# Where four reductions and four PSUM evacuations stand among the first FFN chunks of a gated-mix kernel

## The chip, the cores and the metric

The kernel runs on one core of one Trainium2 chip. The metric is the device time of one execution in microseconds. The median of four runs before the change is 179.18 us, from 178.49 to 179.32. One more execution was taken with the hardware profiler; every line of a profile in this text comes from that execution, and its times count from the start of its span.

Five engines work side by side, each through its own instructions in order: TensorE (PE), which multiplies matrices into PSUM, VectorE (DVE), ScalarE (ACT), GpSimd (POOL) and SyncE (SP), whose queue starts most of the transfers. They wait for each other by semaphores. Weight loads of PE are listed apart as PEld.

## The reference

For 2048 tokens x of width 512, a linear attention block a and a gated FFN b are mixed per token:

```python
x = A_x
g = _sigmoid((x * gate_w).sum(-1, keepdims=True))
a = _A_ref(x, A_wqkv, A_wo)
b = _B_ref(x, B_w1, B_w3, B_w2)
return g * a + (1 - g) * b
```

The attention has 32 heads of 16, with phi(t) = t + 1 where t > 0 and exp(t) elsewhere, plus 1e-6. It is linear: `kv` is the sum over tokens of phi(k) times v, `z` the sum of phi(k), and the output `o` of a token is `num / den`, with `num` = phi(q) times kv and `den` = phi(q) times z for each head, followed by the product with `wo`. The FFN is silu(x w1) * (x w3), times w2, with 1376 hidden units.

## The kernel before

Tokens are cut into four blocks of 512 (`tb` 0 to 3), each into four tiles of 128 (`tt`). The hidden units are ten chunks of 128 (`fc` 0 to 9) and a remainder of 96. The work has three stages.

First, for all 16 tiles, phi(k) is made (`emit_k`) and the products XP of x and phi(k) are added up in four PSUM banks, tags XP0 to XP3 of the pool psX. POOL adds up the phi(k) tiles (`pks`), from which z is made.

Second, block 0 is prepared, in the part around the change: phi(q) (`emit_q`, tiles `pq`), the remainder (`emit_rem`), the small matrix `kvT_sb`, and from it W, the product of kv and wo. PE makes W in the four psX banks as `W_ps0` to `W_ps3`, between chunk 1 and chunk 2 of the FFN; ACT copies them to `W_sb` with a scale (L476).

Third, for each block: ten FFN chunks, then per tile the output `emit_out`, among which the next block's `emit_q`, `emit_rem` and `emit_den` are placed, and then `emit_norm` for that next block.

One FFN chunk (`emit_ffn`, from L312) is: four matmuls gate_ps (L322) and four matmuls up_ps (L330) on PE, `th` = tanh of half of gate_ps on ACT (L335), `gs` = (th + 1) * gate_ps on DVE (L337), and `hT` = up_ps * gs on DVE (L342). A function given as `between` is called between gs and hT.

PSUM sets what waits for what. The pool psM has four banks, which gate_ps and up_ps take in turn: chunk 2 takes again what chunk 0 had, chunk 3 what chunk 1 had. A gate_ps is free when th and gs have read it, an up_ps when hT has. In block 0, chunks 4 and 6 don't use psM but the psX banks, by the table in L317: chunk 4 takes XP2 and XP3, so `W_ps2` and `W_ps3` must have been evacuated before it, and chunk 6 takes XP0 and XP1, so `W_ps0` and `W_ps1` before that. Chunk 5 then takes chunk 2's banks, chunk 7 chunk 3's, chunk 8 chunk 5's and chunk 9 chunk 7's.

The denominator (`emit_den`, L226) is, per tile, a product qz of pq and z on POOL (L228), into one of three buffers, and a reduction to 32 sums on DVE (L231). `emit_norm` (L281) makes rden from the four sums of a block with three DVE operations (L284, L287, L288), then eight products pqn on POOL (L297, three buffers) and four transposing transfers on SP's queue into pqT (L307). The first matmuls of each output tile (L363) read pqT and W_sb.

The order on PE is written out throughout (`manual_schedule`, L153). On DVE it is written out from L414 to L476, which covers chunks 0 to 2 of block 0; behind that, and on the other engines, a scheduler places the instructions. `emit_norm(0)` is called after chunk 5 (L480), and the scheduler puts its three DVE operations at the gs and hT of chunks 3 and 4.

Of the kernel before, what the change touches and what calls it, by code (L numbers as in the profile page):

```python
# [8 lines left out]
ACT = mybir.ActivationFunctionType  # L9
ALU = mybir.AluOpType  # L10
AX = mybir.AxisListType
ENG = mybir.EngineType
FP32 = mybir.dt.float32
# [4 lines left out]
def kernel(  # L18
# [12 lines left out]
    nc = tc.nc  # L31
    P = nc.NUM_PARTITIONS

    Bb, S, D = A_x.shape
# [7 lines left out]
    TPB = TB // P  # L42
    FC = F // P
# [5 lines left out]
    NG = P // G  # L49
# [41 lines left out]
        out=xT[:, :, TF * P : TB], in_=x2d[TF * P : TB, :], transpose=True  # L91
    )
    for tb in range(1, NTB):
        dq.dma_start(
            out=xT[:, :, tb * TB : (tb + 1) * TB], in_=x2d[tb * TB : (tb + 1) * TB, :],
# [7 lines left out]
    with nc.allow_non_contiguous_dma(reason="one gate weight per partition and chunk"):  # L103
        dq.dma_start(
            out=wr_sb[:, :, 2 * FR : NR], in_=gate_w.rearrange("(kc d o) -> d kc o", d=P, o=1)
        )
    dq.dma_start(out=wv_sb[:], in_=wqkv_r[:, :, 2 * D : 3 * D])
    for fsl in (slice(0, FM // 2), slice(FM // 2, FM)):
# [13 lines left out]
        out=bm, in_=bm, pattern=[[-Dh, HPC], [0, Dh]], compare_op=ALU.is_ge, fill=0.0,  # L122
# [3 lines left out]
        out=bm, in_=bm, pattern=[[Dh, HPC], [0, Dh]], compare_op=ALU.is_ge, fill=0.0,  # L126
# [4 lines left out]
    W_sb = consts.tile([P, KC, D], BF16, name="W_sb")  # L131
# [24 lines left out]
    psX = ctx.enter_context(tc.tile_pool(name="psX", bufs=1, space=bass.MemoryType.PSUM))  # L156
# [55 lines left out]
    def emit_q(tb, tt, pool, tag):  # L212
        t = tb * TPB + tt
        ts_tok = slice(t * P, (t + 1) * P)
        if tt == 0:
            st[tb, "pq"] = blk.tile([P, TPB, D], BF16, tag="pq", name="pq")
            st[tb, "den"] = blk.tile([P, TPB, H], FP32, tag="den", name="den")
        q_ps = pool.tile([P, D], FP32, tag=tag, name="q_ps")
        for kc in range(KC):
            nc.tensor.matmul(  # L220
                q_ps[:], lhsT=xT[:, kc, ts_tok], rhs=wq_sb[:, kc, :],
                start=(kc == 0), stop=(kc == KC - 1),
            )
        phi(st[tb, "pq"][:, tt, :], q_ps[:])

    def emit_den(tb, tt):  # L226
        qz = work.tile([P, D], FP32, tag="qz", name="qz")
        nc.gpsimd.tensor_tensor(  # L228
            out=qz[:], in0=st[tb, "pq"][:, tt, :], in1=z_sb[:], op=ALU.mult
        )  # L230
        nc.vector.tensor_reduce(  # L231
            out=st[tb, "den"][:, tt, :], in_=qz[:].rearrange("p (h d) -> p h d", d=Dh),
            axis=AX.X, op=ALU.add,
        )
# [38 lines left out]
    def emit_omg(tb):  # L273
        om = work.tile([P, TPB], FP32, tag="om", name="om")
        nc.vector.tensor_scalar(  # L275
            out=om[:], in0=st[tb, "el"][:], scalar1=2.0, scalar2=2.0, op0=ALU.mult,
            op1=ALU.add,
        )
        nc.vector.reciprocal(out=omg[:, tb * TPB : (tb + 1) * TPB], in_=om[:])
# [32 lines left out]
    def emit_ffn(tb, fc, between=None):  # L312
        tok_sl = slice(tb * TB, (tb + 1) * TB)
        fsl = slice(fc * P, (fc + 1) * P)
        if fc == 0:
            st[tb, "hT"] = blk.tile([P, FC, TB], BF16, tag="hT", name="hT")
        aside = {4: ("XP2", "XP3"), 6: ("XP0", "XP1")}.get(fc) if tb == 0 else None  # L317
        gate_ps = (psX if aside else psM).tile(
            [P, TB], FP32, tag=aside[0] if aside else "mm", name="gate_ps"
        )  # L320
        for kc in range(KC):
            nc.tensor.matmul(  # L322
                gate_ps[:], lhsT=w1_sb[:, kc, fsl], rhs=xT[:, kc, tok_sl],
                start=(kc == 0), stop=(kc == KC - 1),
            )
        up_ps = (psX if aside else psM).tile(
            [P, TB], FP32, tag=aside[1] if aside else "mm", name="up_ps"
        )
        for kc in range(KC):
            nc.tensor.matmul(  # L330
                up_ps[:], lhsT=w3_sb[:, kc, fsl], rhs=xT[:, kc, tok_sl],
                start=(kc == 0), stop=(kc == KC - 1),
            )
        th = work.tile([P, TB], BF16, tag="th", name="th")
        nc.scalar.activation(out=th[:], in_=gate_ps[:], func=ACT.Tanh, scale=0.5)  # L335
        gs = work.tile([P, TB], BF16, tag="gs", name="gs")
        nc.vector.scalar_tensor_tensor(  # L337
            out=gs[:], in0=th[:], scalar=1.0, in1=gate_ps[:], op0=ALU.add, op1=ALU.mult
        )
        if between:  # L340
            between()
        nc.vector.tensor_tensor(  # L342
            out=st[tb, "hT"][:, fc, :], in0=up_ps[:], in1=gs[:], op=ALU.mult
        )
# [69 lines left out]
    with tc.manual_schedule(engines={ENG.DVE}):  # L414
        Q = 32
        NB = D // Q
        zt = consts.tile([P, NB, Q], FP32, name="zt")
        nc.vector.transpose(out=zt[:].rearrange("p b f -> p (b f)"), in_=pks[:])
        w = Q // 2
        while w >= 1:  # L420
            nc.gpsimd.tensor_add(zt[:, :, 0:w], zt[:, :, 0:w], zt[:, :, w : 2 * w])
            w //= 2
        zq = zt[:, :, 0]
        z_up = consts.tile([P // 2, NB], FP32, name="z_up")
        z_h = consts.tile([P // 2, NB], FP32, name="z_h")
        z_hi = consts.tile([Q, NB], FP32, name="z_hi")
        z_col = consts.tile([P, NB], FP32, name="z_col")
        nc.gpsimd.tensor_copy(z_up[:], zq[P // 2 : P, :])
        nc.gpsimd.tensor_add(z_h[:], zq[0 : P // 2, :], z_up[:])
        nc.gpsimd.tensor_copy(z_hi[:], z_h[Q : 2 * Q, :])  # L430
        for b in range(P // Q):
            nc.gpsimd.tensor_add(z_col[b * Q : (b + 1) * Q, :], z_h[0:Q, :], z_hi[:])
        for dc in range(KC):
            if dc % 2 == 0:
                nc.scalar.activation(out=XP_sb[:, dc, :], in_=XP_ps[dc][:], func=ACT.Copy)
            else:
                nc.vector.tensor_copy(out=XP_sb[:, dc, :], in_=XP_ps[dc][:])

        emit_q(0, TPB - 1, psM, "mm")
        emit_rem(0, 0, psM, "mm")  # L440
        emit_rem(0, 1, psM, "mm")
        nc.vector.transpose(
            out=z_sb[:].rearrange("p (b f) -> p b f", f=Q),
            in_=z_col[:, :, None].to_broadcast([P, NB, Q]),
        )
        kvT_ps = psX.tile([P, KC, P], FP32, tag="XP0", name="kvT_ps")
        for c in range(KC):
            csl = slice(c * P, (c + 1) * P)
            for dc in range(KC):
                nc.tensor.matmul(  # L450
                    kvT_ps[:, c, :], lhsT=wv_sb[:, dc, csl], rhs=XP_sb[:, dc, csl],
                    start=(dc == 0), stop=(dc == KC - 1),
                )
        nc.vector.tensor_tensor(
            out=kvT_sb[:], in0=kvT_ps[:],
            in1=blockmask[:, None, :].to_broadcast([P, KC, P]), op=ALU.mult,
        )

        emit_omg(0)
        for fc in range(3):  # L460
            if fc == 0:
                emit_ffn(0, fc)
                continue
            emit_den(0, 2 * fc - 2)
            emit_ffn(0, fc, between=lambda: emit_den(0, 2 * fc - 1))
            if fc == 1:
                W_ps = [psX.tile([P, D], FP32, tag=f"XP{i}", name=f"W_ps{i}") for i in range(NG)]
                for i in range(NG):
                    gsl = slice(i * G, (i + 1) * G)
                    for c in range(KC):  # L470
                        nc.tensor.matmul(
                            W_ps[i][c * G : (c + 1) * G, :], lhsT=kvT_sb[gsl, c, gsl],
                            rhs=wo_sb[gsl, c, :], start=True, stop=True,
                        )
            for i in ((2, 3) if fc == 1 else (0, 1)):
                nc.scalar.activation(out=W_sb[:, i, :], in_=W_ps[i][:], func=ACT.Copy, scale=2.0)  # L476

    for fc in range(3, FC):
        emit_ffn(0, fc)
        if fc == TPB + 1:  # L480
            emit_norm(0)
# [47 lines left out]
```

## Time and profile before

| What | Value |
| --- | --- |
| median of four runs | 179.18 us |
| runs | 178.49, 179.17, 179.32, 179.19 us |
| the profiled execution | 179.29 us |
| its span, first to last instruction | 177.6 us |
| mean granted TensorE clock | 0.998 of full speed |
| DVE reductions L231 | 16, 684 ns each |
| ACT evacuations of W, L476 | 4, 603 ns each |
| ACT tanh L335 | 40, 598 ns each |
| POOL products L228 / L297 | 16, 1160 ns each / 32, 626 ns each |

The profiled execution lasts 1.69 us longer than its span, which counts from the first to the last instruction. Busy time of an engine is the sum of its instructions' lengths; instructions of one engine can overlap at their ends, since one starts before the last one's result is written. So the distance from start to start says how fast an engine goes on, and the length says when a result is there.

The span in 40 slices of 4.4 us shows how full each engine is, in tenths:

```profile
PE   8999999999999999999999999999999999999994
DVE  0397667899999837498786375978754669786000
ACT  3542323476442334343333333342443333331222
POOL 6087765689155323263003232720032328100000
```

Chunks 0 to 9 of block 0 lie from 38.7 to 56.9 us, slices 9 to 13 (counted from 1), where DVE is at nine tenths or more.

### The profile page before, as it was taken

The numbers are of one execution on the slowest core, as the hardware profiler recorded it, in microseconds if no ns is written. First come the engines' busy times: TensorE is split into PE (matmuls) and PEld (weight loads), VectorE is DVE, ScalarE is ACT, GpSimd is POOL, SyncE is SP. The second block draws the span as 40 slices with busy tenths as digits, with TensorE's granted clock in tenths as the row PEclk, the third lists the DMA queues.
The fourth block names the chain that finished last, engine by engine and source line by source line (L and its number), as shares of the span: only waits on it lengthen the run. The fifth ranks groups of instructions, "written<-read, shape, count | busy, mean of one in ns | idle before, by whom it ended". The sixth has DMA issues, their size and how long they took to land.

```text
span 177.6 us, 2513 instructions
## 1 busy us (share of the span) xinstructions
PE 174.0 (98%) x895; PEld 83.8 (47%) x895; DVE 118.6 (67%) x204; ACT 65.3 (37%) x123; POOL 66.2 (37%) x96
## 2 busy tenths in 40 slices
PE   8999999999999999999999999999999999999994
PEld 4444444474444545444454544444545444444463
DVE  0397667899999837498786375978754669786000
ACT  3542323476442334343333333342443333331222
POOL 6087765689155323263003232720032328100000
PEclk9999999999999999999999999999999999999999
DMA  5999999901004010123000111240001012300002
GB/s 181 243 283 241 279 363 362 339 24 22 17 0 111 7 48 30 44 59 89 0 4 7 37 37 37 59 94 2 0 7 55 23 51 63 70 0 0 30 33 59
DMA packets 30380, 15.14 MB, mean 85 GB/s; under 512 B 20928, under 2 KB 30240, under 8 KB 30368
## 3 DMA queue, kind: packets, MB, share of 16 engines
q1 hardware_dynamic: 29952, 14.67, 29.8%
q10 hardware_dynamic: 416, 0.31, 0.6%
q8 instruction: 7, 0.11, 0.3%
q14 instruction: 5, 0.04, 0.1%
HBM read 8.42 MB, written 2.10 MB: 59 GB/s over the span
## 4 chain that ended last, share of the span: by engine, by line
PE 94%; DVE 4%; issue 1%; DVEq 0%
PE o_ps L372 19%; PE up_ps L330 18%; PE gate_ps L322 18%; PE o_ps L363 8%; PE XP L207 8%; PE q_ps L220 8%; PE k_ps L187 6%; PE r_ps L244 3%; PE k L187 2%; PE o_ps L367 2%; PE warm L164 2%; DVE hT L342 1%; DVE gs L337 1%; DVE om L275 1%; PE xTp L177 0%
## 5 line engine op out<-in xcount | busy, mean ns | idle before, releaser
L330 PE MATMUL up_ps<-xT,w_sb 128*128 128x512 bf16 x160 | 41.1, 379 | 0.2 <-DVE hT L342 0.2
L322 PE MATMUL gate_ps<-xT,w_sb 128*128 128x512 bf16 x160 | 41.1, 379 | 0.0
L228 POOL TENSOR_TENSOR qz<-pq,z_sb 128x512 f32<-128x512 bf16 x16 | 18.5, 1160 | 57.0 <-DVE pq L148 57.0
L335 ACT ACTIVATE th<-gate_ps 128x512 bf16<-128x512 f32 x40 | 23.9, 598 | 39.5 <-PE gate_ps L322 39.1
L372 PE MATMUL o_ps<-w_sb,hT 128*128 128x512 bf16 (+3 forms) x180 | 37.5, 355 | 0.0
L337 DVE SCALAR_TENSOR_TENSOR gs<-th,gate_ps 128x512 bf16<-128x512 bf16 x40 | 27.2, 681 | 5.4 <-ACT th L335 5.1
L342 DVE TENSOR_TENSOR hT<-up_ps,gs 128x512 bf16<-128x512 f32 x40 | 27.6, 691 | 3.7
L145 DVE TENSOR_SCALAR phi_m<-phi_e 128x512 bf16<-128x512 bf16 x32 | 13.6, 425 | 21.7 <-ACT phi_e L143 21.5
L372 PEld LDWEIGHTS <-hT 128*128 128x128 bf16 x180 | 16.9, 98 | 17.8
L330 PEld LDWEIGHTS <-w_sb 128*128 128x128 bf16 x160 | 15.6, 98 | 19.2 <-issue 0.4
L322 PEld LDWEIGHTS <-w_sb 128*128 128x128 bf16 x160 | 15.5, 98 | 18.6 <-issue 0.2
L297 POOL TENSOR_TENSOR pqn<-pq,rden 128x256 bf16<-128x256 bf16 x32 | 19.0, 626 | 13.8 <-DVE rden L288 13.1
L377 ACT ACTIVATE o_out<-o_ps,omg 128x512 bf16<-128x512 f32 x15 | 10.3, 687 | 28.9 <-PE o_ps L372 28.9
L197 POOL TENSOR_TENSOR pks<-pks,pk_sb 128x512 f32<-128x512 f32 x15 | 17.4, 1161 | 7.3 <-DVE pk_sb L148 6.7
L363 PE MATMUL o_ps<-W_sb,pqT 128*128 128x512 bf16 (+3 forms) x72 | 16.8, 355 | 0.0
L220 PE MATMUL q_ps<-wq_sb,xT 128*128 128x512 bf16 x64 | 16.4, 379 | 0.0
L207 PE MATMUL XP<-pk_sb,x_sb 128*128 128x512 bf16 x64 | 16.3, 379 | 0.0
L231 DVE TENSOR_REDUCE den<-qz 128x32 f32<-128x512 f32 x16 | 10.9, 684 | 7.9 <-POOL qz L228 7.8
L143 ACT ACTIVATE phi_e<-k_ps 128x512 bf16<-128x512 f32 x12 | 7.2, 597 | 14.4 <-PE k_ps L187 14.4
L143 ACT ACTIVATE phi_e<-q_ps 128x512 bf16<-128x512 f32 x16 | 9.6, 597 | 7.8 <-PE q_ps L220 7.8
L187 PE MATMUL k_ps<-wk_sb,xT 128*128 128x512 bf16 x48 | 12.3, 379 | 0.0
L148 DVE SCALAR_TENSOR_TENSOR pq<-q_ps,phi_m 128x512 bf16<-128x512 f32 x16 | 11.1, 691 | 0.5
(60 smaller groups left out, 119.4 us busy)
## 6 DMA issues: line engine op xcount, KB each, us to landing
w_sb<-in_B_w_dram SPq DMA_DIRECT2D x4, 640.0 KB, 7.5
out_dram<-o_out SPq DMA_DIRECT2D x15, 128.0 KB, 1.7
w_sb<-in_B_w_dram SPq DMA_DIRECT2D x1, 1280.0 KB, 12.2
x_sb<-in_A_x_dram SPq DMA_DIRECT2D x2, 512.0 KB, 4.3
x_sb<-in_A_x_dram SPq DMA_DIRECT2D x1, 768.0 KB, 5.1
wq_sb<-in_A_wqkv_dram SPq DMA_DIRECT2D x1, 512.0 KB, 4.9
wv_sb<-in_A_wqkv_dram SPq DMA_DIRECT2D x1, 512.0 KB, 6.4
wo_sb<-in_A_wo_dram SPq DMA_DIRECT2D x1, 512.0 KB, 9.5
```

The costliest lines, as they stand in the source:

```text
L187: nc.tensor.matmul(k_ps[:], lhsT=xT[:, kc, t * P : (t + 1) * P], rhs=wk_sb[:, kc, :], start=(kc == 0), stop=(kc == KC - 1),)
L207: nc.tensor.matmul(XP_ps[dc][:], lhsT=x_sb[:, t, dc * P : (dc + 1) * P], rhs=pk_sb[:, t, :], start=(t == 0), stop=(t == NT - 1),)
L220: nc.tensor.matmul(q_ps[:], lhsT=xT[:, kc, ts_tok], rhs=wq_sb[:, kc, :], start=(kc == 0), stop=(kc == KC - 1),)
L228: nc.gpsimd.tensor_tensor(out=qz[:], in0=st[tb, "pq"][:, tt, :], in1=z_sb[:], op=ALU.mult)
L297: nc.gpsimd.tensor_tensor(out=pqn[:].rearrange("p (i c e) -> p c i e", i=NG, c=KC)[:, :, :, dsl], in0=st[tb, "pq"][:, tt, :].rearrange("p ...
L322: nc.tensor.matmul(gate_ps[:], lhsT=w1_sb[:, kc, fsl], rhs=xT[:, kc, tok_sl], start=(kc == 0), stop=(kc == KC - 1),)
L330: nc.tensor.matmul(up_ps[:], lhsT=w3_sb[:, kc, fsl], rhs=xT[:, kc, tok_sl], start=(kc == 0), stop=(kc == KC - 1),)
L335: nc.scalar.activation(out=th[:], in_=gate_ps[:], func=ACT.Tanh, scale=0.5)
L337: nc.vector.scalar_tensor_tensor(out=gs[:], in0=th[:], scalar=1.0, in1=gate_ps[:], op0=ALU.add, op1=ALU.mult)
L342: nc.vector.tensor_tensor(out=st[tb, "hT"][:, fc, :], in0=up_ps[:], in1=gs[:], op=ALU.mult)
L363: nc.tensor.matmul(o_ps[:], lhsT=st[tb, "pqT"][:, c, tsl], rhs=W_sb[:, c, a:b], start=(c == 0), stop=False,)
L372: nc.tensor.matmul(o_ps[:], lhsT=st[tb, "hT"][:, fc, tsl], rhs=w2_sb[:, fc, a:b], start=False, stop=(fc == FC - 1),)
```

## The change

Before, DVE makes two sums in each of chunks 1 and 2: one ahead of the chunk's gs, one between its gs and hT. After, it makes one in each of chunks 1 to 4, between gs and hT. The stretch in which DVE's order is written out is extended to the end of chunk 4, and from chunk 1 on ACT's order is written out too. The four evacuations of W, which before stood in a row ahead of chunk 2's tanh, are put at: `W_ps2` after chunk 1's tanh, `W_ps3` and `W_ps0` after chunk 2's, `W_ps1` after chunk 3's. `emit_norm(0)` is still called after chunk 5; in the built program its three DVE operations now stand in chunks 5 and 6: the addition between gs and hT of chunk 5, the reciprocal between that hT and chunk 6's gs, the product between chunk 6's gs and hT. PE, POOL and SP keep the order of their instructions, and every count and size stays the same.

```diff
         emit_omg(0)
-        for fc in range(3):
-            if fc == 0:
-                emit_ffn(0, fc)
-                continue
-            emit_den(0, 2 * fc - 2)
-            emit_ffn(0, fc, between=lambda: emit_den(0, 2 * fc - 1))
+        emit_ffn(0, 0)
+
+    with tc.manual_schedule(engines={ENG.DVE, ENG.Activation}):
+        W_ps = [psX.tile([P, D], FP32, tag=f"XP{i}", name=f"W_ps{i}") for i in range(NG)]
+
+        def emit_W_sb(i):
+            nc.scalar.activation(out=W_sb[:, i, :], in_=W_ps[i][:], func=ACT.Copy, scale=2.0)
+
+        for fc in range(1, TPB + 1):
+            emit_ffn(0, fc, between=lambda: emit_den(0, fc - 1))
             if fc == 1:
-                W_ps = [psX.tile([P, D], FP32, tag=f"XP{i}", name=f"W_ps{i}") for i in range(NG)]
                 for i in range(NG):
...
-            for i in ((2, 3) if fc == 1 else (0, 1)):
-                nc.scalar.activation(out=W_sb[:, i, :], in_=W_ps[i][:], func=ACT.Copy, scale=2.0)
-
-    for fc in range(3, FC):
+            for i in {1: (2,), 2: (3, 0), 3: (1,)}.get(fc, ()):
+                emit_W_sb(i)
+
+    for fc in range(TPB + 1, FC):
         emit_ffn(0, fc)
         if fc == TPB + 1:
             emit_norm(0)
```

## The prediction

> **What bounds the kernel now.** I read the page's busy shares first, then the waits, then each engine's timeline around the one wait inside the stream, last the tile pqT, whose making is moved.
>
> ```profile
> span 177.6 us, 2513 instructions
> PE 174.0 (98%) x895; PEld 83.8 (47%) x895; DVE 118.6 (67%) x204; ACT 65.3 (37%) x123; POOL 66.2 (37%) x96
> ```
>
> TensorE (PE) is busy for 174.0 of 177.6 us. The matmul count doesn't change, so the change can only act through the time in which PE stands still. The waits list, for PE alone, has two entries:
>
> ```profile
> PE warm L164 <- PEq L513: 0.8, 1, 0.8
> PE up_ps L330 <- DVE hT L342: 0.2, 1, 0.2
> ```
>
> The first is the start. The second is one wait, of the up projection for VectorE's (DVE's) hT product. PE's timeline (start, length, what) places it in chunk 3:
>
> ```profile
> 42.62 1.04 PE L322 MATMUL gate_ps<-xT,w_sb 128*128 128x512 bf16 x4
> 43.50 1.03 PE L330 MATMUL up_ps<-xT,w_sb 128*128 128x512 bf16 x4
> 44.36 1.03 PE L322 MATMUL gate_ps<-xT,w_sb 128*128 128x512 bf16 x4
> 45.54 1.02 PE L330 MATMUL up_ps<-xT,w_sb 128*128 128x512 bf16 x4 [0.15 <-DVE hT L342]
> ```
>
> Groups of four start 0.86 to 0.87 apart wherever nothing waits (43.50 to 44.36; 45.54 to the next at 46.41). Here 45.54 - 44.36 = 1.18. So PE lost 1.18 - 0.865 = 0.32 us. The bracket says 0.15 because a group's listed end (44.36 + 1.03 = 45.39) lies behind the start that the next one could have had. DVE in the same stretch, and near its end:
>
> ```profile
> 42.42 0.69 DVE L342 TENSOR_TENSOR hT<-up_ps,gs 128x512 bf16<-128x512 f32 x1
> 43.03 0.68 DVE L231 TENSOR_REDUCE den<-qz 128x32 f32<-128x512 f32 x1
> 43.62 0.68 DVE L337 SCALAR_TENSOR_TENSOR gs<-th,gate_ps 128x512 bf16<-128x512 bf16 x1
> 44.22 0.68 DVE L231 TENSOR_REDUCE den<-qz 128x32 f32<-128x512 f32 x1
> 44.81 0.68 DVE L342 TENSOR_TENSOR hT<-up_ps,gs 128x512 bf16<-128x512 f32 x1
> ...
> 55.54 0.68 DVE L337 SCALAR_TENSOR_TENSOR gs<-th,gate_ps 128x512 bf16<-128x512 bf16 x1
> 56.32 0.69 DVE L342 TENSOR_TENSOR hT<-up_ps,gs 128x512 bf16<-128x512 f32 x1
> ```
>
> up_ps of chunk 3 gets the PSUM buffer of chunk 1's up_ps, free when hT1 ends: 44.81 + 0.68 = 45.49, and PE starts at 45.54. DVE has no gap before it; two sums (den) stand between hT0 and hT1, each moving what follows by 0.60. The last two lines show that an hT directly behind its own gs starts 0.78 later, against 0.60 where another operation stands between.
>
> ScalarE (ACT), with four evacuations of W ahead of chunk 2's tanh, though that gate_ps ends at 42.62 + 1.04 = 43.66:
>
> ```profile
> 42.70 2.06 ACT L476 ACTIVATE W_sb<-W_ps 128x512 bf16<-128x512 f32 x4 [0.60 <-PE W_ps L471]
> 44.63 0.63 ACT L335 ACTIVATE th<-gate_ps 128x512 bf16<-128x512 f32 x1
> ```
>
> **The change, part by part.** Chunk numbers follow the names: hT3 is chunk 3's.
>
> *Sums.* hT1 has one reduction ahead instead of two: gs1 at 43.03, den0 at 43.62, hT1 at 44.22 to 44.90. th1 (41.50 + 0.60 = 42.10) and the first qz (40.34 + 1.16 = 41.50) are long there. up_ps3 is due at 44.36 + 0.865 = 45.22 and finds its buffer free 0.32 before, 0.27 after the 0.04 to 0.05 from hT's end to PE's start. Wait gone: -0.32 on PE (bounds -0.15, the bracket, and -0.32; I take -0.32, since starts at an even pitch carry the stream).
>
> *What is due next.* gs2 would stand at 44.82, before only at 46.00. Without the ACT part it would wait for th2 (44.63 + 0.63 = 45.26): 0.44 more. With it, ACT does one evacuation at 42.70, th2 at 43.69 to 44.29, then W3 and W0 (2.06 for four is 0.49 a step) until 45.3, th3 at 45.42 to 46.02, W1 until 46.6, and th4 after gate_ps4, at about 47.15. All are in time for DVE at 0.60 a step: den1 45.41, hT2 46.01, gs3 46.60, den2 47.20, hT3 47.79, gs4 48.39, den3 48.98, hT4 49.58, gs5 50.17. PE's other releases, each due 0.32 earlier than before: gate_ps4 and up_ps4 (46.09, 46.95) need W2 and W3, done by 44.8; gate_ps5 (47.81) gs2, 45.50; up_ps5 (48.68) hT2, 46.69; gate_ps6 and up_ps6 (49.54, 50.40) W0 and W1, 46.6; gate_ps7 (51.27) gs3, 47.28; up_ps7 (52.13) hT3, 48.47. No wait. Price: 0.
>
> *The end of the stretch.* From chunk 5 on DVE has gs5 50.17, the norm's addition (L284), hT5 50.96, reciprocal 51.57 (0.86 to the next), gs6 52.43, product with el (L288) 52.97 to 53.25, hT6 53.17, gs7 53.77, hT7 54.55, hT9 57.31 (before 57.71). That is 0.40 less than before, because the sums and the norm now stand between gs and hT in two more chunks: 2 x (0.78 - 0.60) = 0.36. The tightest release is gate_ps9, due 55.04 - 0.32 = 54.72, which needs gs7: 53.77 + 0.68 = 54.45. Margin 0.27, against 0.20 before (gs7 54.16 + 0.68, gate_ps9 55.04).
>
> The Trainium skill, page "VectorE: DVE Perf Modes", section "The DRAIN you can't avoid", speaks against that 0.36: the pipe is flushed after every operation, a semaphore costs nothing extra, so order alone would save no DVE time. The rows here differ (0.60 against 0.78). By the rule hT9 would stay near 57.7; the PE sum is the same by both, since hT1 has one operation fewer ahead in either.
>
> *The norm, moved.* Its three DVE operations now follow den3, and L288 ends at 53.25 instead of 50.58 + 0.28 = 50.86: 2.39 later. With it go eight POOL products pqn and four transposes on SP's queue:
>
> ```profile
> L363 PEld LDWEIGHTS <-pqT x16: 97/98/98, 58.2 to 71.7; 128*128 128x128 bf16 x16
> L307 SPq DMA_TRANSPOSE pqT<-pqn x4: 1212/1217/1221, 52.2 to 56.1; - x4
> ...
> DMA to landing us min/median/max: 2.3/2.4/2.4
> 50.94 1.21 POOL L297 TENSOR_TENSOR pqn<-pq,rden 128x256 bf16<-128x256 bf16 x2 [5.99 <-DVE rden L288]
> ```
>
> The first piece was issued at 52.17; now 54.56, landing at 54.56 + 2.4 = 56.96. Its reader, the first o_ps (L363), loads weights at 58.2 - 0.32 = 57.88: cover 0.9 us. If the cover is gone, PE waits for every further us. The later pieces land by 56.1 + 2.39 + 2.4 = 60.9, and the second is due at 62.24. POOL's next work (next block's qz, 59.56 - 0.32 = 59.24) stands behind pqn, which ends at 55.91 + 2.39 = 58.30; SP's next transposes (61.24 - 0.32 = 60.92) behind an issue that ends at 57.32 + 2.39 = 59.71. Price: 0.
>
> *Small things.* qz3 waits for den0, whose end moves from 43.71 to 44.30: done at 45.5, needed by den3 at 48.98. The weight load of up_ps4 gets a wait on PE's own count, for a W matmul of 42.7, due at 46.9. Such a wait stands at the second r_ps of a block and not at the first: from q_ps to o_ps (L363) it is 56.93 to 58.46 without and 65.80 to 67.33 with it, 1.53 both times. Price: 0. Evacuation counts and lengths stay.
>
> **Sum.** The profiled execution took 179.29: 177.6 of span and 1.69 around it. 177.6 - 0.32 + 1.69 = 178.97. It lies 0.11 above the median of the runs (179.18), so 178.86 is the forecast. That is -0.18%; 0.3% (0.54 us) is about what a measurement of this kernel can tell from no change.
>
> **Rivals.**
> 1. *The wait moves on.* DVE slips by more than 0.27 on the way to gs7, and gate_ps9 waits in up_ps3's place. For: DVE is at 7.88 of 8.40 us from 50.0 to 58.4, hardly any slack. Against: the margin was 0.20 before and held. Time: up to the whole 0.32 given back, 179.18.
> 2. *pqT comes late: slower.* The first o_ps waits for the transposes, once the first piece lands after 57.88. If L288 slips by one chunk and one reduction more (1.73 + 0.60 = 2.33), it lands at 59.29, PE waits 1.41, and the net is +1.09: 180.27. It is slower by 0.3% from a landing 0.86 beyond 57.88. For: only 0.9 us of cover remain of 3.6, and nothing after chunk 9 hides it. Against: no DVE operation ahead of L288 has a late input.
> 3. *The stall was worth more.* The timed runs spread from 178.49 to 179.32, more than the 0.32 found. If the wait is longer in the usual run than in the profiled one, removing it brings 0.7: 178.5. Against: nothing in the trace shows a second wait, and the profiled run is as slow as the usual.
> 4. *The new order isn't what runs.* On DVE, ACT and PE it is written out in this stretch, and the norm is placed behind it; against it speaks only that the scheduler still places the norm. It counts under 1.
>
> **How the numbers follow.** Forecast 0.60, rival 1 (with 4) 0.16, rival 2 0.07, rival 3 0.17. Faster by over 0.3%: most of rival 3 (0.15) and the part of the forecast that the runs' spread carries there (0.09): 0.24. Slower: rival 2 and 0.03 of spread: 0.10. Within: 0.66. The range goes down to the lowest run less about a third of the gain (178.49 - 0.11, 178.38) and up to the highest run with nothing gained and a little of rival 2 (179.32 + 0.08, 179.40): 178.38 to 179.40.
>
> **What would show it.** Right: PE's waits list without up_ps <- hT; up_ps3 0.86 to 0.87 behind gate_ps3; hT1 near 44.2, th2 near 43.7; L288 near 53 and the first pqT transpose issued near 54.6; the first o_ps near 58.0; the span near 177.3. Wrong: a bracket at gate_ps9 or up_ps9 (rival 1), at the first L363 naming the transposes or pqn (rival 2), or a span shorter by over 0.54 with PE's pitch unchanged (rival 3). Any PE time lost beyond chunk 9 would break the sum, which takes it that all later work only moves by 0.32.

## The result, and the profile after

The changed kernel takes 178.59 us (median of 54 runs, 177.99 to 179.32) against 178.95 for the kernel before in the same sessions (78 runs, 178.30 to 179.64). The ratio is 0.998, 95% interval 0.9972 to 0.9988: 0.36 us faster, clear of noise and within the 0.3% that was named as a measurement's reach.

The waits of PE in the changed kernel, over the whole span, are one line. It is the start; the wait of up_ps for hT is not there any more:

```profile
PE warm L164 <- PEq L516: 0.8, 1, 0.8
```

PE's timeline around the place where the wait was (start, length, what):

```profile
41.73 1.04 PE L322 MATMUL gate_ps<-xT,w_sb 128*128 128x512 bf16 x4
42.60 1.03 PE L330 MATMUL up_ps<-xT,w_sb 128*128 128x512 bf16 x4
43.47 1.03 PE L322 MATMUL gate_ps<-xT,w_sb 128*128 128x512 bf16 x4
44.33 1.03 PE L330 MATMUL up_ps<-xT,w_sb 128*128 128x512 bf16 x4
```

The last row is chunk 3's up_ps (up_ps3 in what follows), 0.86 behind its gate_ps where it was 1.18. DVE and ACT in the same stretch:

```profile
42.18 0.68 DVE L337 SCALAR_TENSOR_TENSOR gs<-th,gate_ps 128x512 bf16<-128x512 bf16 x1
42.78 0.68 DVE L231 TENSOR_REDUCE den<-qz 128x32 f32<-128x512 f32 x1
43.38 0.69 DVE L342 TENSOR_TENSOR hT<-up_ps,gs 128x512 bf16<-128x512 f32 x1
43.99 0.68 DVE L337 SCALAR_TENSOR_TENSOR gs<-th,gate_ps 128x512 bf16<-128x512 bf16 x1
```

```profile
41.88 0.60 ACT L466 ACTIVATE W_sb<-W_ps 128x512 bf16<-128x512 f32 x1 [0.67 <-PE W_ps L474]
42.80 0.60 ACT L335 ACTIVATE th<-gate_ps 128x512 bf16<-128x512 f32 x1 [0.33 <-PE gate_ps L322]
43.30 1.08 ACT L466 ACTIVATE W_sb<-W_ps 128x512 bf16<-128x512 f32 x2
```

hT1 ends at 43.38 + 0.69 = 44.07, 0.26 ahead of up_ps3. Chunk 2's tanh runs as soon as its gate_ps is there, and gs2 follows hT1 without a gap.

The two profiled spans differ by 1.2 us (177.6 and 176.4), three times the difference of the medians. Most of it lies ahead of the change: chunk 0's first matmul starts at 38.71 before and at 37.82 after, 0.89 earlier, though nothing there was edited (the last section says where the difference arises). So all comparisons below are made from that start. The two ends of the stretch, chunk 0's first gate_ps and the next block's first q_ps, in the kernel before and then in the changed one:

```profile
38.71 1.03 PE L322 MATMUL gate_ps<-xT,w_sb 128*128 128x512 bf16 x4
56.77 1.03 PE L220 MATMUL q_ps<-wq_sb,xT 128*128 128x512 bf16 x4
```

```profile
37.82 1.03 PE L322 MATMUL gate_ps<-xT,w_sb 128*128 128x512 bf16 x4
55.55 1.03 PE L220 MATMUL q_ps<-wq_sb,xT 128*128 128x512 bf16 x4
```

From the one to the other PE takes 56.77 - 38.71 = 18.06 us before and 55.55 - 37.82 = 17.73 after: 0.33 less. Behind it the span has 120.83 left before (177.6 - 56.77) and 120.85 after. The gain was made in this stretch, and all of it was kept.

### The profile page after: what moved, and what is told of

It reads as the page before. It is cut to its first block, busy times and chain, and to the rows that moved or that the text cites. A ratio compares the mean times of both kernels' runs of the same rounds, so it can differ in the third digit from the quotient of the medians.

```text
span 176.4 us, 2513 instructions
## 1 busy us (share of the span) xinstructions
PE 172.9 (98%) x895; PEld 83.3 (47%) x895; DVE 118.5 (67%) x204; ACT 65.3 (37%) x123; POOL 66.3 (38%) x96
## 4 chain that ended last, share of the span: by engine, by line
PE 98%; DVE 0%; issue 0%
PE gate_ps L322 20%; PE o_ps L372 20%; PE up_ps L330 20%; PE o_ps L363 8%; PE q_ps L220 8%; PE XP L207 8%; PE k_ps L187 6%; PE r_ps L244 3%; PE k L187 2%; PE o_ps L367 2%; PE warm L164 2%; PE kvT_ps L450 1%; PE xTp L177 0%; PE W_ps L474 0%; DVE o_last L381 0%
## 5 line engine op out<-in xcount | busy, mean ns | idle before, releaser
L342 DVE TENSOR_TENSOR hT<-up_ps,gs 128x512 bf16<-128x512 f32 x40 | 27.6, 691 | 3.5
L363 PE MATMUL o_ps<-W_sb,pqT 128*128 128x512 bf16 (+3 forms) x72 | 16.8, 355 | 0.0
```

The source lines that it names most:

```text
L342: nc.vector.tensor_tensor(out=st[tb, "hT"][:, fc, :], in0=up_ps[:], in1=gs[:], op=ALU.mult)
L363: nc.tensor.matmul(o_ps[:], lhsT=st[tb, "pqT"][:, c, tsl], rhs=W_sb[:, c, a:b], start=(c == 0), stop=False,)
```

## The experiments

The table gives, for each run, PE's time from chunk 0's first gate_ps to the next block's first q_ps (17.73 where nothing waits), and the time against the kernel before on the same chip.

| Run | PE stretch, us | median, us | before, us | ratio (95%) |
| --- | --- | --- | --- | --- |
| before | 18.06 | | | |
| after | 17.73 | 178.59 | 178.95 | 0.998 (0.9972 to 0.9988) |
| e1_sums_only | 17.99 | 178.83 | 179.10 | 0.9991 (0.9974 to 1.0009) |
| e2_act_only | 18.10 | 179.28 | 179.10 | 1.0008 (0.9992 to 1.0025) |
| e3_sum_ahead_of_gs | 18.74 | 179.37 | 179.10 | 1.0025 (1.0009 to 1.0041) |
| e5_extra_sum | 18.28 | 179.01 | 179.10 | 1.0009 (0.9994 to 1.0024) |
| e4_norm_late | 17.74, then 1.73 lost | 180.50 | 178.87 | 1.0089 (1.0057 to 1.012) |
| e6_sum_ahead_chunk1 | 18.12 | 179.58 (one run) | 178.87 | |
| e7_shifted | 17.94 | 179.07 (one run) | 178.87 | |

Times of single runs spread by over 1 us, so for differences of 0.1 to 0.3 us the starts in the profile decide, and the ratios only have to agree with them. The stretch of each run is that of its one profiled execution. In the text a run is called by the start of its label (e1 for e1_sums_only).

### The order of the sums alone

```diff
-            for i in {1: (2,), 2: (3, 0), 3: (1,)}.get(fc, ()):
+            for i in {1: (0, 1, 2, 3)}.get(fc, ()):
                 emit_W_sb(i)
```

> The changed order of the sums alone; the four evacuations of W stay in a row ahead of chunk 2's tanh, as before. Theory (DVE has no slack to gs7, so both parts are needed): no wait at up_ps3, since hT1 has one sum ahead; but th2 ends about 1.0 us later than in the changed kernel, gs2 starts 0.45 to 0.5 later, and everything behind it on DVE too, so that gate_ps9 waits for gs7 by 0.2 to 0.3 us; time 0.0 to 0.1 us below the kernel before. Rival (the ACT part is idle cover): no wait on PE anywhere, time 0.3 to 0.4 us below the kernel before.

PE's timeline, chunks 8 and 9:

```profile
53.32 1.03 PE L330 MATMUL up_ps<-xT,w_sb 128*128 128x512 bf16 x4
54.45 1.02 PE L322 MATMUL gate_ps<-xT,w_sb 128*128 128x512 bf16 x4
```

and DVE's, where gs2 comes late and gs7 with it:

```profile
44.76 0.69 DVE L337 SCALAR_TENSOR_TENSOR gs<-th,gate_ps 128x512 bf16<-128x512 bf16 x1 [0.34 <-ACT th L335]
...
53.72 0.68 DVE L337 SCALAR_TENSOR_TENSOR gs<-th,gate_ps 128x512 bf16<-128x512 bf16 x1
```

No wait at up_ps3; gate_ps9 starts 1.13 behind up_ps8 instead of 0.86: 0.27 lost, right behind gs7's end at 53.72 + 0.68 = 54.40. Of the 0.33 only 0.07 is left (18.06 - 17.99). The list of waits has no entry for gate_ps9: the group before has its listed end at 53.32 + 1.03 = 54.35, so most of the 0.27 looks busy, and only the starts show it. Theory as stated: the sums remove the wait, and without the ACT part DVE's delay puts it six chunks further on. The timed runs alone don't tell theory from rival (the interval, 0.9974 to 1.0009, holds both); the starts do.

### The order on ACT alone

```diff
+        with tc.manual_schedule(engines={ENG.Activation}):
...
+            for fc in range(1, 3):
+                emit_den(0, 2 * fc - 2); emit_ffn(0, fc, between=lambda: emit_den(0, 2 * fc - 1))
...
+                for i in {1: (2,), 2: (3, 0, 1)}.get(fc, ()):
+                    emit_W_sb(i)
```

> The ACT order alone: tanh of chunk 2 ahead of three of the four evacuations, the sums two in chunk 1 and two in chunk 2 as before (the norm's first addition moves from behind chunk 3's gs to ahead of it). Theory (the sums ahead of hT1 make the wait): up_ps3 still waits, 0.32 us from start to start beyond the pitch, and the time equals the kernel before within 0.1 us. Rival (the evacuations ahead of the tanh made the wait): no wait at up_ps3, 0.3 us below the kernel before.

The wait stays, in the waits of PE:

```profile
PE up_ps L330 <- DVE hT L342: 0.2, 1, 0.2
```

On the timeline up_ps3 starts 1.19 behind gate_ps3 (45.65 and 44.46), 0.32 beyond the pitch. The stretch is 18.10, the time that of the kernel before within its interval. So the evacuations ahead of the tanh were no cause of the wait. In PE's stretch either part alone is worth next to nothing (0.07 and -0.04); only both together give 0.33.

### Each sum ahead of its gs

```diff
-            emit_ffn(0, fc, between=lambda: emit_den(0, fc - 1))
+            emit_den(0, fc - 1); emit_ffn(0, fc)
```

> The changed kernel with each of the four sums ahead of its chunk's gs instead of between gs and hT; counts and ACT order as in the changed kernel. Theory (an hT directly behind its gs starts 0.78 after it, not 0.60, so each sum between them saves 0.18): gs7 0.7 to 0.85 us later than in the changed kernel against PE, so gate_ps9 waits 0.4 to 0.6 us; no wait at up_ps3; time 0.1 to 0.3 us above the kernel before. Rival (order within DVE costs nothing, the count alone matters): gs7 where it is in the changed kernel, no wait, 0.3 to 0.4 us below the kernel before.

PE's waits and, below them, DVE's timeline of chunks 1 and 2:

```profile
PE gate_ps L322 <- DVE gs L337: 0.5, 1, 0.5
PE up_ps L330 <- DVE hT L342: 0.2, 1, 0.2
```

```profile
42.99 0.68 DVE L337 SCALAR_TENSOR_TENSOR gs<-th,gate_ps 128x512 bf16<-128x512 bf16 x1
44.17 0.69 DVE L342 TENSOR_TENSOR hT<-up_ps,gs 128x512 bf16<-128x512 f32 x1 [0.50 <-PE up_ps L330]
44.77 0.68 DVE L231 TENSOR_REDUCE den<-qz 128x32 f32<-128x512 f32 x1
45.37 0.68 DVE L337 SCALAR_TENSOR_TENSOR gs<-th,gate_ps 128x512 bf16<-128x512 bf16 x1
46.15 0.69 DVE L342 TENSOR_TENSOR hT<-up_ps,gs 128x512 bf16<-128x512 f32 x1
```

gate_ps9 starts 1.50 behind up_ps8 (55.04 and 53.54), 0.64 lost. gs7, counted from chunk 0's gate_ps, starts at 54.31 - 38.02 = 16.29, against 52.94 - 37.82 = 15.12 in the changed kernel. Of these 1.17, 4 x (0.78 - 0.60) = 0.72 are the four places, in chunks 1, 2, 3 and 6, where an hT now stands directly behind its gs (45.37 to 46.15 is one), and 0.40 are a gap that no theory had: hT1 starts 1.18 behind gs1, not 0.78. It brings back the wait at up_ps3 as well (0.32). The profile blames up_ps, but chunk 1's up_ps had ended at 40.61 + 1.03 = 41.64. The rival, that only the count of operations matters, falls: the counts are the same, the three hT without that gap start 0.78 behind their gs as well, and the ratio's interval lies above 1. Whether the timed runs all have the gap is not known.

### A second reduction ahead of hT1

```diff
-            emit_ffn(0, fc, between=lambda: emit_den(0, fc - 1))
+            emit_ffn(0, fc, between=lambda: emit_den(0, fc - 1, fc == 1))
...
-        nc.vector.tensor_reduce(
+        for _ in range(1 + extra): nc.vector.tensor_reduce(
```

> The changed kernel with chunk 1's reduction made twice (the same sums written again), so that again two reductions stand ahead of hT1. Theory (0.60 us per reduction on DVE, all of it on the way to up_ps3): the wait at up_ps3 is back with 0.3 us, and up to 0.1 more at gate_ps9; time within 0.1 us of the kernel before. Rival (the wait came from the place of the sums in chunk 2 or from ACT): no wait at up_ps3, time as the changed kernel, 0.3 to 0.4 below.

The wait is back, and more than expected: up_ps3 starts 1.36 behind gate_ps3, 0.50 lost, and gate_ps9 0.05 late. The waits of PE:

```profile
PE up_ps L330 <- DVE hT L342: 0.3, 1, 0.3
```

DVE's timeline has both reductions in one row:

```profile
42.92 1.40 DVE L231 TENSOR_REDUCE den<-qz 128x32 f32<-128x512 f32 x2
44.24 0.68 DVE L342 TENSOR_TENSOR hT<-up_ps,gs 128x512 bf16<-128x512 f32 x1
```

The second reduction moved hT1 by 0.72, not 0.60 (the pair starts at 42.92, hT1 at 44.24, 1.32 later; in the changed kernel hT1 starts 0.60 behind its sum), and the slack before it was 0.21 (0.26 less the 0.05 from an hT's end to PE's start): 0.72 - 0.21 = 0.51. That a reduction ahead of hT1 makes the wait is shown; its price of 0.60 was too low for one that writes the same sums again. The time can't be told from the kernel before, as expected.

### The norm late

```diff
-        for fc in range(1, TPB + 1):
-            emit_ffn(0, fc, between=lambda: emit_den(0, fc - 1))
+        for fc in range(1, FC):
+            emit_ffn(0, fc, between=(lambda: emit_den(0, fc - 1)) if fc <= TPB else None)
+            if fc == 7: emit_norm(0)
...
-    for fc in range(TPB + 1, FC):
-        emit_ffn(0, fc)
-        if fc == TPB + 1:
-            emit_norm(0)
```

> The changed kernel with the norm's three DVE operations in a row behind hT7 instead of among chunks 5 and 6, so that rden is ready about 2.65 us later (L288 would end at about 55.1 on the changed kernel's clock, 52.43 in it). It tests rival 2 of the prediction, the price of late pqT pieces. Theory (cover of 0.86 us: in the changed kernel the first transpose is issued at 53.74, lands 2.4 later at 56.14, and the first o_ps loads at 57.0): PE waits 1.6 to 2.0 us at the first L363, nothing else; time 1.2 to 1.7 us above the kernel before, ratio 1.007 to 1.010. Rival (other waits or later slack hide it): less than 0.5 us, time within 0.3% of the kernel before.

PE's waits in this run, and below them the tile pqT in the changed kernel (weight loads, transposes and time to landing):

```profile
PE o_ps L363 <- DMA pqT<-pqn: 1.8, 1, 1.8
```

```profile
L363 PEld LDWEIGHTS <-pqT x16: 97/98/98, 57.0 to 70.5; 128*128 128x128 bf16 x16
L307 SPq DMA_TRANSPOSE pqT<-pqn x4: 1211/1216/1216, 53.7 to 57.7; - x4
...
DMA to landing us min/median/max: 2.3/2.4/2.4
```

In the changed kernel the first piece lands at 53.7 + 2.4 = 56.1, 0.9 ahead of its load at 57.0. In this run the first transpose is issued at 57.51, 18.55 behind chunk 0's gate_ps (38.96), against 15.92 (53.74 - 37.82): 2.63 later, of which 0.9 is cover. What is left is 1.73. The list says 1.8, but it counts to a later matmul, for only three of the first four L363 are recorded there; the matmul behind them (L367) starts 60.82 - 38.96 = 21.86 behind chunk 0's gate_ps, against 57.95 - 37.82 = 20.13: 1.73 lost, as the sum has it. The kernel before is slower than the changed one by 0.33, so against it 1.4 us are due in the time; 1.63 were measured (180.50 against 178.87; the interval is 1.0 to 2.1). Nothing is given back behind the wait: from that L367 to the end of the span it is 118.4 us in both. The change did spend most of a cover: it went from 3.6 us to 0.9.

### The gap at hT1

One kernel has the sum ahead of gs in chunk 1 alone:

```diff
-            emit_ffn(0, fc, between=lambda: emit_den(0, fc - 1))
+            emit_den(0, 0) if fc == 1 else None; emit_ffn(0, fc, between=(lambda: emit_den(0, fc - 1)) if fc > 1 else None)
```

> The changed kernel with only chunk 1's sum ahead of gs1, the other three between gs and hT. In e3_sum_ahead_of_gs hT1 started 1.18 us after its gs1, 0.40 more than the 0.78 that other chunks show, and that, not the 0.78, made a wait at up_ps3. Theory A (the 0.40 belongs to this place in the program): hT1 again 1.1 to 1.2 after gs1, wait of about 0.3 us at up_ps3. Theory B (an accident of that one execution): hT1 0.78 after gs1, no wait at up_ps3. In both, the wait of gate_ps9 is at most 0.3 us, half of e3's 0.64 or less, since three sums still stand between.

The other has besides, in `emit_omg`:

```diff
-        nc.vector.reciprocal(
+        for _ in range(2 if tb == 0 else 1): nc.vector.reciprocal(
```

> As e6_sum_ahead_chunk1, with the reciprocal of omg for block 0 made twice, so that every later DVE instruction stands one place further back in DVE's program, and starts 0.1 to 0.2 us later. If the 0.40 us gap hangs on the count of instructions before it (a refill of DVE's instruction buffer), it moves to the instruction that now holds the old place (gs1 or the event wait before hT1), or goes; if it hangs on hT1 and what hT1 waits for, it stays between gs1 and hT1.

DVE's timeline of e6:

```profile
43.85 0.68 DVE L337 SCALAR_TENSOR_TENSOR gs<-th,gate_ps 128x512 bf16<-128x512 bf16 x1
45.04 0.69 DVE L342 TENSOR_TENSOR hT<-up_ps,gs 128x512 bf16<-128x512 f32 x1 [0.51 <-PE up_ps L330]
```

and of e7, with one more instruction ahead:

```profile
43.73 0.68 DVE L337 SCALAR_TENSOR_TENSOR gs<-th,gate_ps 128x512 bf16<-128x512 bf16 x1
44.52 0.69 DVE L342 TENSOR_TENSOR hT<-up_ps,gs 128x512 bf16<-128x512 f32 x1
```

In e6 hT1 starts 1.19 behind gs1, with a wait of 0.33 at up_ps3 (1.20 behind gate_ps3): theory A. In e7 it is 0.79, and PE has no listed wait at all (its gate_ps3 is 0.2 late, for gs1 itself came later). Where e6 lost the 0.40 its trace shows at L342 (DVEq is DVE's sequencer, which takes the wait for gs1 ahead of hT1):

```profile
L342 DVEq EVENT_SEMAPHORE  x1: 21/21/21, 44.6 to 44.6; - x1
L342 DVE TENSOR_TENSOR hT<-up_ps,gs x1: 692/692/692, 45.0 to 45.0; 128x512 bf16<-128x512 f32 x1
```

The wait was over at 44.6, in time (gs1 ends at 43.85 + 0.68 = 44.53), and hT1 started only 0.4 later. So the gap isn't the accident of one execution, for e3 and e6 both have it, and it isn't a late input of hT1. It went when one more instruction stood ahead. But in e7 gs1 also came 0.2 us later, so this run alone doesn't tell the place in DVE's program from the time; the last section has what the traces add. In e6 the loss at gate_ps9 is 0.05, against 0.64 with all four sums ahead.

## Why the prediction was right

The direction, the size and the place were right: 0.32 forecast, 0.33 found in PE's stretch, 0.36 in the medians. By its steps, each time counted from chunk 0's first gate_ps (38.71 in the forecast, 37.82 measured):

- *The wait and its 0.32.* Right, and so was the choice between 0.15 and 0.32: starts at an even pitch carry the stream. e1, e2 and e5 show that the second reduction ahead of hT1 made it.
- *hT1, th2, gs2.* Forecast 5.51, 4.98 and 6.11; measured 5.56, 4.98 and 6.17.
- *"Without the ACT part ... 0.44 more" for gs2.* e1 has gs2 at 6.58, 0.41 more. The prediction priced that delay but not where it would end: rival 1, the wait moved to gate_ps9, is what the sums alone give, down to its place and 0.27 us. In the full change rival 1 didn't occur.
- *The end of the stretch.* Here a term was mis-sized. The margin at gate_ps9 was to be 0.27 and is 0.21 (gs7 ends at 52.94 + 0.68 = 53.62, gate_ps9 starts at 53.83), hardly more than the 0.20 before. DVE gains 0.32 to hT9 (19.00 to 18.68), not 0.40. Most of what is missing lies ahead of the moved sums: hT0 starts at 3.76, where it was 3.71. From hT0 to hT9 DVE takes 14.92 after 15.29, so the two places that were counted with 0.36 gave 0.37.
- *The order on DVE has a price.* e3 decides between the row and the rule that the prediction drew from a page against it (the Trainium skill, "VectorE: DVE Perf Modes", "The DRAIN you can't avoid"): with equal counts, the order cost 0.72 us by gs7. The measurement holds: of these 128x512 operations, one that waits for the one directly ahead of it starts 0.78 behind it, not 0.60. What falls is the conclusion that order saves nothing; the page's own measurement, the same eight copies with and without semaphores, was not repeated here.
- *The norm moved at no cost.* Right: the first transpose was forecast at 15.85 and issued at 15.92; the cover is 0.9 as said. e4 shows rival 2's price beyond it, one for one.
- *The wait on PE's own count at up_ps4's weight load.* Nothing: gate_ps4 to gate_ps5 is 46.92 - 45.19 = 1.73, two pitches.
- *Rival 3.* Not so: 0.36 us were gained (interval 0.2 to 0.5), not 0.7, and PE's stretch says the same. The profiles have another source for the spread that spoke for it, the start of the kernel.
- *The absolute time.* 178.86 forecast, 178.59 measured: the base, not the step. The four runs shown before had a median 0.23 above that of 78.

No experiment points to a kernel faster than the changed one: PE's list has no wait left behind the kernel's first matmul, and from chunk 2 to the next block its groups of four start 0.86 to 0.87 apart.

## What to carry to other kernels

When one engine is full, look at its start-to-start distances, not only at its list of waits: 0.27 us were lost at gate_ps9 in e1 without an entry. Where a saturated helper engine feeds it, removing one wait helps only as far as the helper's slack to its next deadline, so walk the order through to the last deadline before pricing either half of an edit alone. And on DVE put independent work between an operation and the one that needs its result: it filled 0.18 us a time here.

## What the runs showed of the hardware that was not expected

*A gap of 0.40 us at one place of DVE's program.* In e3 and e6 hT1 starts 1.18 to 1.19 behind gs1; with one more instruction ahead (e7) it is 0.79. In the changed kernel hT1 stands at the same place of the program, but a reduction runs while it is made ready, and there is no gap. One more reading of the traces speaks for the place, and not the time. In the first 10 us from chunk 0's start the queue q14, which the profile lists as `instruction`, moves three packets of 8 KB in each of the nine kernels. The first and the third keep their time within 0.5 us; the second starts anywhere from 5.0 to 7.0, and it goes with this place. In the changed kernel, e1, e3, e4 and e6, which have hT1 at this place directly behind its wait, it starts 1.2 to 1.3 us behind the end of that wait; in the kernel before, e2 and e7, where hT1 stands one place later, it starts 0.4 to 0.7 ahead of that end (e5 has no such wait). The Trainium skill, "Runtime: NRT & Kernel Launch", "Instruction fetch mechanics", says that an engine refills its instructions in blocks and that crossing a block's boundary is mostly hidden. That would fit: the crossing is seen only when the instruction at the boundary comes directly behind a wait. The page gives 16 KiB for such a block, where these packets have 8. The profile doesn't say which engine the packet is for, and what the engine does in the 0.40 us was not measured, so the cause stays open.

*The start of the kernel moves all that follows by up to 1.1 us.* In the kernel before, the tile k of the first matmuls reads (durations as least, median and most, then first and last start):

```profile
L187 PE MATMUL k<-wk_sb,xT x16: 379/379/631, 4.5 to 8.6; 128*128 128x512 bf16 x16
```

and in the changed kernel:

```profile
L187 PE MATMUL k<-wk_sb,xT x16: 379/379/390, 4.5 to 7.7; 128*128 128x512 bf16 x16
```

The first of these matmuls start 0.43 us apart in the profiled execution of the kernel before (4.53, 4.96, 5.38, 5.81), twice the 0.22 of the later ones, and that puts everything behind them 0.85 later (from the first k to the first XP 4.33 against 3.48). In the changed kernel's profile they start 0.21 to 0.23 apart from the first on. It isn't the change that does this, for no edit touches this part: from the first k to the first XP the nine profiles take between 3.47 (e5) and 4.51 (e6), and from there to chunk 0, which starts between 37.82 and 38.96, they all take 29.85 or 29.86. The mean granted clock doesn't tell them apart: it is 1.000 in e4, which takes 4.43, and 0.998 in the kernel before, which takes 4.33. Why the first matmuls are slow in some executions was not measured, and the timed runs don't show their start. But the 54 runs of the changed kernel alone reach from 177.99 to 179.32. So two single executions of this kernel can differ by more than the change is worth, and neither span nor one time tells it; the distance from chunk 0 to the next block does.
